# Early expert's w1: second halves of the columns split at the early slot instead of during attention; first tile's last low-part products moved

## The chip, the cores and the metric

One of the eight cores of a Trainium2 chip runs the kernel. The metric is the device time of one execution in microseconds (us), the median of three runs, lower being better. TensorE (PE) multiplies, VectorE (DVE), ScalarE (ACT) and GpSimd (POOL) do the work on elements, SyncE (SP) issues most transfers.

## The reference

Attention with a soft cap on the scores, for 8 batches, 12 heads, 448 positions and a head width of 64, is followed by a layer of experts on the 3584 rows of 768 that it yields; each row goes through the one expert of eight that its gate picks.

```python
scores = cap * np.tanh(np.matmul(q, k.transpose(0, 1, 3, 2)) / 8 / cap)
attn = softmax(scores)
x = (attn @ v).transpose(0, 2, 1, 3).reshape(3584, 768)
logits = x @ w_gate + modality_bias[modality_id]
e_idx, gate_w = argmax(logits), max(softmax(logits))
out[e_idx == e] = gate_w * (relu(x @ w1[e]) @ w2[e])     # w1: 768 x 1024, w2: 1024 x 768
```

## The kernel before

All matrix operands are split into a high part in a short float format (a cast on ScalarE) and the low rest (a subtraction on VectorE), and each product is made of three: high by high, high by low, low by high.

Attention (`attention`, L446) goes through 24 quads of four heads, three to a batch, each in four stages r = 0 to 3; a hand-written table, `ORDER`, says which steps of which quad are issued in a stage, and ScalarE does seven tanh (L532) and seven exp (L539) in each quad. A 25th round (i = 24, table `LAST`) finishes the last quad. Beside this the rows found so far are routed (`route`, L223): gate values, then the rank of each row within its expert by a matmul over counts (L257), a position from it (`pos`, L271), and four indirect puts by GpSimd that write row numbers and gate values to a table in DRAM, `mapd` (L284).

After four batches the expert with most rows is picked: the early expert. Its first 384 rows, all found in batches 0 to 5, are gathered during attention, and its first weights w1 (six tiles of 128x1024) are loaded and split there too: `load_part`, `hi_part` and `lo_part` (L665 to L682) work on twelve half tiles of 128x512, in the order left half, right half of tile 0, then of tile 1 and so on. Ten are split in quads 14 to 23, one in each stage r = 1, the last two at i = 24 and in `before`.

So the experts' part can start with a slot of 384 rows while the last batch is still being routed: the early slot. A slot (`run_slot`, L973) is a first layer (`ffn1`, L917; eight steps f, each 18 products of 128x384 into one bank, then relu into `hh` on ScalarE and its rest `hl` on VectorE), and a second (`ffn2`, L948; for each of three tiles of 128 rows and two halves of the columns, eight f with three products each into one bank `py`, which ScalarE scales into `ot`). Step f of the first layer needs columns 128 f to 128 f + 127 of all six w1 tiles, f of the second needs w2 tile f. Between the steps of the early slot's first layer stand hooks: `before`, `last` and `ranks` finish the last batch and its routing, `order` makes the plan of the slots that follow (`slots`, L325: a chain of some fifty short VectorE operations from `cnt`, L333, to `metai`, L395, and on to `plani`, L431), and `load_w2` loads and splits w2 tiles. Raw tiles of 128x1024 rotate through four buffers, so a load waits for the subtraction of the tile four back. Three w2 tiles are loaded ahead of the slot (`nstage`).

When the puts have landed GpSimd reads the list of the next slot's rows (`mt`, L837) and gathers them (L853, three gathers); TensorE transposes them late in the early slot's second layer (L895). The next slot's w1 is loaded and split from the second tile of the second layer on. Names in the traces: `raw` an unsplit weight tile, `ah`/`al` the parts of w1, `bh`/`bl` those of w2. On SyncE loads stand in the order of the program; on VectorE, ScalarE and TensorE too where an instruction is given to `pin`, the others being placed by a scheduler.

## Time and profile before

| | before |
|---|---|
| median of 3 runs | 838.93 us (838.35 to 839.43) |
| the profiled execution's own time | 840.97 us |
| its span | 839.3 us |
| TensorE busy | 823.2 us (98%), 5605 instructions |
| ScalarE busy | 528.1 us (63%) |
| VectorE busy | 518.7 us (62%) |
| GpSimd busy | 131.0 us (16%) |
| loads | 151.98 MB, mean 181 GB/s |

The span is that of one profiled execution; around it lie 1.7 us that the profile does not show. A share of busy time is a mean over the attention, where VectorE and ScalarE are nearly as full as TensorE, and the experts' part, where they are half empty. Rows of a timeline give the start, the duration, the engine, the line, the operation with its tiles, and in brackets the idle time of the engine just before with what ended it.

### The profile page before, as it was taken

The numbers are of one execution on the slowest core, as the hardware profiler recorded it, in microseconds if no ns is written. First come the engines' busy times: TensorE is split into PE (matmuls) and PEld (weight loads), VectorE is DVE, ScalarE is ACT, GpSimd is POOL, SyncE is SP. The second block draws the span as 40 slices with busy tenths as digits, with TensorE's granted clock in tenths as the row PEclk, the third lists the DMA queues.
The fourth block names the chain that finished last, engine by engine and source line by source line (L and its number), as shares of the span: only waits on it lengthen the run. The fifth ranks groups of instructions, "written<-read, shape, count | busy, mean of one in ns | idle before, by whom it ended". The sixth has DMA issues, their size and how long they took to land. (4 is left out here: it accounts for less than half of the span.)

```text
span 839.3 us, 15177 instructions
## 1 busy us (share of the span) xinstructions
PE 823.2 (98%) x5605; PEld 647.6 (77%) x5605; DVE 518.7 (62%) x987; ACT 528.1 (63%) x693; POOL 131.0 (16%) x155
## 2 busy tenths in 40 slices
PE   8999999999999999999999999999999999999995
PEld 3445454454545454999999999999999999999984
DVE  7788989899999998855344453444534335326510
ACT  7999999999999998345344453434534245335610
POOL 1000212020202024235020020200202002011101
PEclk9999999999999999999999999999999999999999
DMA  6565574858585855668366461654716547138743
GB/s 204 156 208 176 188 202 163 227 150 235 164 244 160 241 166 127 176 184 270 151 190 225 127 232 61 212 197 144 244 56 209 176 145 249 58 109 269 248 181 117
DMA packets 54649, 151.98 MB, mean 181 GB/s; under 512 B 9752, under 2 KB 18720, under 8 KB 54562
## 3 DMA queue, kind: packets, MB, share of 16 engines
q1 hardware_dynamic: 45200, 117.78, 45.4%
q0 software_dynamic: 9216, 33.10, 11.4%
q8 instruction: 47, 0.77, 0.4%
q14 instruction: 40, 0.33, 0.1%
q10 hardware_dynamic: 146, 0.00, 0.0%
HBM read 113.91 MB, written 22.40 MB: 162 GB/s over the span
## 5 line engine op out<-in xcount | busy, mean ns | idle before, releaser
L532 ACT ACTIVATE th<-sc,isc 128x896 f32<-128x896 f32 x168 | 161.1, 1003 | 8.3 <-PE sc L518 5.2
L932 PE MATMUL ph<-x,ah 128*128 128x384 f32 (+1 forms) x480 | 156.5, 326 | 1.4 <-ACT ot L967 1.0
L936 PE MATMUL ph<-x,al 128*128 128x384 f32 (+1 forms) x480 | 155.8, 325 | 0.0
L933 PE MATMUL ph<-x,ah 128*128 128x384 f32 (+1 forms) x480 | 155.8, 325 | 0.0
L962 PE MATMUL py<-bh,hh 128*128 128x384 f32 x448 | 151.0, 337 | 0.0
L962 PE MATMUL py<-bh,hl 128*128 128x384 f32 x448 | 149.9, 334 | 0.0
L962 PE MATMUL py<-bl,hh 128*128 128x384 f32 x448 | 149.8, 334 | 0.0
L539 ACT ACTIVATE pt<-th,cabs 128x896 f32<-128x896 f32 x144 | 142.1, 1042 | 0.0
L942 ACT ACTIVATE hh<-ph 128x384 fp32r<-128x384 f32 (+1 forms) x80 | 37.4, 469 | 131.7 <-PE ph L936 122.3
L552 PE MATMUL xT<-pt,va 128*64 128x448 f32 x576 | 118.8, 548 | 0.7 <-DVE xs L652 0.7
L870 DVE TENSOR_TENSOR bl<-raw,bh 128x768 fp32r<-128x768 f32 x80 | 74.3, 956 | 60.6 <-ACT bh L869 56.8
L943 DVE SCALAR_TENSOR_TENSOR hl<-ph,hh 128x384 fp32r<-128x384 f32 (+1 forms) x80 | 42.0, 528 | 106.5 <-ACT hh L942 105.1
L967 ACT ACTIVATE ot<-py,mt 128x384 f32<-128x384 f32 x56 | 32.5, 581 | 98.8 <-PE py L962 59.6
L932 PEld LDWEIGHTS ph<-x,ah 128*128 128x128 f32 x480 | 90.2, 188 | 2.8 <-issue 1.3
L968 POOL DMA_INDIRECT out_dram<-ot,mt x28 | 32.2, 1150 | 380.7 <-ACT ot L967 354.8
L933 PEld LDWEIGHTS ph<-x,ah 128*128 128x128 f32 x480 | 90.2, 188 | 0.0
L936 PEld LDWEIGHTS ph<-x,al 128*128 128x128 f32 x480 | 90.2, 188 | 0.0
L870 DVE TENSOR_TENSOR al<-raw,ah 128x1024 fp32r<-128x1024 f32 x54 | 63.9, 1222 | 35.1 <-ACT ah L869 32.2
L962 PEld LDWEIGHTS py<-bh,hh 128*128 128x128 f32 x448 | 84.1, 188 | 1.2 <-issue 0.7
L962 PEld LDWEIGHTS py<-bl,hh 128*128 128x128 f32 x448 | 84.1, 188 | 0.0
L962 PEld LDWEIGHTS py<-bh,hl 128*128 128x128 f32 x448 | 84.1, 188 | 0.0
L552 PEld LDWEIGHTS xT<-pt,va 128*64 128x64 f32 x576 | 37.1, 136 | 60.8 <-issue 51.4
(201 smaller groups left out, 1211.1 us busy)
## 6 DMA issues: line engine op xcount, KB each, us to landing
raw<-in_w_dram SPq DMA_DIRECT2D x86, 384.0 KB
raw<-in_w_dram SPq DMA_DIRECT2D x60, 512.0 KB
kq<-in_kq_dram SPq DMA_DIRECT2D x47, 448.0 KB
va<-in_v_dram SPq DMA_DIRECT2D x24, 448.0 KB
xd<-xs POOLq DMA_DIRECT2D x24, 448.0 KB
cp<-xT SPq DMA_DIRECT2D x44, 224.0 KB
cp<-gl SPq DMA_DIRECT2D x22, 224.0 KB
raw<-in_w_dram SPq DMA_DIRECT2D x12, 256.0 KB
```

What stands on the lines that cost most here:

```text
L532: pin(nc.scalar.activation(th, sc[:, :, :S], AF.Tanh, scale=self.isc))
L539: pin(nc.scalar.activation(e, th, AF.Exp, scale=self.cabs))
L552: pin(pe.matmul(xT[j * D : (j + 1) * D, :S], va[:, u * D : (u + 1) * D], quads[q]["pt"][t, i][:, j], start=t == i == 0, stop=t == 1 and i ...
L870: b = self.nc.vector.tensor_tensor(lo, raw, hi, op=ALU.subtract)
L932: nc.tensor.matmul(ph[:, :w], hi[:, fs], self.x[k][:, 0, :w], start=first, stop=False)
L933: nc.tensor.matmul(ph[:, :w], hi[:, fs], self.x[k][:, 1, :w], start=False, stop=False)
L936: nc.tensor.matmul(ph[:, :w], lo[:, fs], self.x[k][:, 0, :w], start=False, stop=last)
L942: nc.scalar.activation(hh[:, f, :w], acc, AF.Relu)
L943: nc.vector.scalar_tensor_tensor(hl[:, f, :w], acc, 0.0, hh[:, f, :w], op0=ALU.max, op1=ALU.subtract)
L962: nc.tensor.matmul(py[:, :HALF], self.h[a][:, f, rows], self.w2s[f][c][:, cs], start=i == 0, stop=i == 3 * FC - 1,)
L967: nc.scalar.mul(ot[:, cs], py[:, :HALF], mt[:, t, 1:2])
L968: self.last_out = nc.gpsimd.indirect_dma_start(self.out, bass.IndirectOffsetOnAxis(ap=mt.bitcast(I32)[:, t, 0:1], axis=0), ot, None, bound ...
```

## The change

In attention only the six left halves of the w1 tiles are loaded and split, in quads 15, 16, 18, 19, 21 and 22 (`PARTS`); quads 14, 17, 20 and 23 do nothing of it. The right halves are loaded after quad 23, two to a raw tile, and split at i = 24 and in the hooks `before`, `last` and a new one, `behind`. The rank matmul of the last batch moves from behind step f = 2 to behind f = 4. One w2 tile is loaded ahead in place of three; the others are loaded from the hooks behind f = 3 and 4 on.

In the second layer, the first tile of every slot makes the high-by-low products (w2's low part) of f = 5, 6 and 7 of its first half not in their place, but behind nine products of the other half; both banks are open meanwhile.

```diff
@@ -662,24 +662,31 @@
                     )
 
 
+            def part(n):
+                k, late = n % KC, n // KC
+                src = raws[KC + k // 2][:, k % 2 * 512 : k % 2 * 512 + 512] if late else raws[k]
+                return src, (t[:, late * 512 : late * 512 + 512] for t in self.w1s[k])
+
             def hi_part(n):
-                k, cs = n // 2, slice(n % 2 * 512, n % 2 * 512 + 512)
-                pin(nc.scalar.copy(self.w1s[k][0][:, cs], raws[n]))
+                src, (hi, lo) = part(n)
+                pin(nc.scalar.copy(hi, src))
 
             def lo_part(n):
-                k, cs = n // 2, slice(n % 2 * 512, n % 2 * 512 + 512)
-                hi, lo = self.w1s[k]
-                pin(nc.vector.tensor_tensor(lo[:, cs], raws[n], hi[:, cs], op=ALU.subtract))
+                src, (hi, lo) = part(n)
+                pin(nc.vector.tensor_tensor(lo, src, hi, op=ALU.subtract))
 
             def early_lo(i):
-                if 0 <= i - FIRST < 2 * KC - 2:
-                    lo_part(i - FIRST)
-
-            def load_part():
-                k, cs = len(raws) // 2, slice(len(raws) % 2 * 512, len(raws) % 2 * 512 + 512)
-                raw = self.up.tile([128, FF], F32, name="raw", tag="raw", bufs=RAWS)[:, :512]
-                self.load(raw, self.w1[ds(e, 1), k * 128 : (k + 1) * 128, cs].rearrange("o p f -> (o p) f"))
-                raws.append(raw)
+                if i in PARTS:
+                    lo_part(PARTS.index(i))
+
+            def load_parts(*ks, late=0):
+                raw = self.up.tile([128, FF], F32, name="raw", tag="raw", bufs=RAWS)
+                for n, k in enumerate(ks):
+                    self.load(
+                        raw[:, n * 512 : n * 512 + 512],
+                        self.w1[ds(e, 1), k * 128 : (k + 1) * 128, late * 512 : late * 512 + 512].rearrange("o p f -> (o p) f"),
+                    )
+                raws.append(raw if late else raw[:, :512])
 
             ORDER = (
                 ((group, 0, (None,)), (pvs, -1), (tot1, -1, 1), (xs, -1, 0), (tot2, -1, 1)),
@@ -708,7 +715,7 @@
                 ((den, -2),),
             )
             PICK, KNOWN = 3, 6
-            FIRST = PICK * NH + 5
+            PARTS = [PICK * NH + u for u in (6, 7, 9, 10, 12, 13)]
             WAYS = {(NQ - 2, 2): B - 2, **{(b * NH + 4, 3): b for b in range(B - 2)}}
             STEPS = [
                 (NQ - 2, 3), *((NQ - 1, r) for r in (0, 0, 1, 1)),
@@ -763,26 +770,35 @@
                         self.early_full(self.ps_r)
                         early = e, self.rows(meta, 0)
                         self.gather(early[1], known=KNOWN * S)
-                    if r == 1 and 0 <= i - FIRST < 2 * KC - 2:
-                        hi_part(i - FIRST)
-                    if r == 1 and 0 <= i - FIRST + 1 < 2 * KC:
-                        load_part()
+                    if r == 1 and i in PARTS:
+                        hi_part(PARTS.index(i))
+                    if r == 1 and i + 1 in PARTS:
+                        load_parts(PARTS.index(i + 1))
                     if (i, r) == (NQ - 1, 3):
                         self.make_x()
+                        for k in range(0, KC, 2):
+                            load_parts(k, k + 1, late=1)
                     if (i, r) == (NQ, 1):
                         self.split_x(*moved[1])
                         self.split_x(*turn_two(4, 5))
-                        hi_part(2 * KC - 2)
-                        lo_part(2 * KC - 2)
+                        hi_part(KC)
+                        hi_part(KC + 1)
+                        lo_part(KC)
+                    if (i, r) == (NQ, 2):
+                        for n in (1, 2):
+                            hi_part(KC + n + 1)
+                            lo_part(KC + n)
             self.raws = [self.load_raw(e, self.w2, k, DM) for k in range(self.nstage)]
 
             def before():
-                hi_part(2 * KC - 1)
+                hi_part(KC + 4)
+                hi_part(KC + 5)
                 tp(NQ - 2, 0)
                 tp(NQ - 2, 1)
                 lt(NQ - 1)
                 rows(NQ - 2, 0)
                 rows(NQ - 2, 1)
+                lo_part(KC + 3)
                 den(NQ - 1)
                 way(B - 1)
 
@@ -791,15 +807,18 @@
                 tp(NQ - 1, 1)
                 for _ in range(3):
                     next(routing[0])
+                lo_part(KC + 4)
+
+            def behind():
+                lo_part(KC + 5)
                 rows(NQ - 1, 0)
                 rows(NQ - 1, 1)
 
             def ranks():
                 for _ in range(2):
                     next(routing[0], None)
-                lo_part(2 * KC - 1)
-
-            return early, ((0, before), (1, last), (2, ranks))
+
+            return early, ((0, before), (1, last), (2, behind), (4, ranks))
 
 
     def moe_pools(self, st):
@@ -951,20 +970,24 @@
         for t in range(n):
             ot = self.lp.tile([128, C * 256], F32, name="ot", tag="late", bufs=3)[:, :DM]
             rows = slice(t * 128, (t + 1) * 128)
-            for half in range(2):
+            steps = [[(half, f, a, c) for f in range(FC) for a, c in ((0, 0), (0, 1), (1, 0))] for half in range(2)]
+            if t == 0:
+                late = [(0, f, 0, 1) for f in range(FC - 3, FC)]
+                steps = [[step for step in steps[0] if step not in late] + steps[1][:9] + late, steps[1][9:]]
+            py, left = [None, None], [3 * FC, 3 * FC]
+            for half, f, a, c in steps[0] + steps[1]:
+                if a == c == 0 and (2 * t + half, f) in at:
+                    at[2 * t + half, f]()
+                if py[half] is None:
+                    py[half] = self.ps_y.tile([128, 512], F32, name="py")
                 cs = slice(half * HALF, (half + 1) * HALF)
-                py = self.ps_y.tile([128, 512], F32, name="py")
-                i = 0
-                for f in range(FC):
-                    if (2 * t + half, f) in at:
-                        at[2 * t + half, f]()
-                    for a, c in ((0, 0), (0, 1), (1, 0)):
-                        nc.tensor.matmul(
-                            py[:, :HALF], self.h[a][:, f, rows], self.w2s[f][c][:, cs],
-                            start=i == 0, stop=i == 3 * FC - 1,
-                        )
-                        i += 1
-                nc.scalar.mul(ot[:, cs], py[:, :HALF], mt[:, t, 1:2])
+                left[half] -= 1
+                nc.tensor.matmul(
+                    py[half][:, :HALF], self.h[a][:, f, rows], self.w2s[f][c][:, cs],
+                    start=left[half] == 3 * FC - 1, stop=left[half] == 0,
+                )
+                if left[half] == 0:
+                    nc.scalar.mul(ot[:, cs], py[half][:, :HALF], mt[:, t, 1:2])
             self.last_out = nc.gpsimd.indirect_dma_start(
                 self.out, bass.IndirectOffsetOnAxis(ap=mt.bitcast(I32)[:, t, 0:1], axis=0), ot, None,
                 bounds_check=NT - 1, oob_is_err=False,
@@ -1252,7 +1275,7 @@
     def build(self):
         tc, nc = self.tc, self.nc
         with ExitStack() as st:
-            self.nstage = RAWS - 1
+            self.nstage = 1
             self.cpool = st.enter_context(tc.tile_pool(name="cpool", bufs=1))
             dram = st.enter_context(tc.tile_pool(name="dram", bufs=1, space=DRAM))
             self.plani = self.cpool.tile([1, 3], I32, name="plani")
@@ -1275,7 +1298,7 @@
                             self.meta = self.slots(rt, self.ps_r, True)
 
                         w2 = lambda at, *ks: (at, lambda: self.load_w2(early[0], self.raws, range(*ks)))
-                        self.run_slots(early, (*late, w2(2, 0, 4), (3, order), *(w2(f, f, f + 1) for f in range(4, FC))))
+                        self.run_slots(early, (*late, w2(3, 0, 2), (3, order), w2(4, 2, 4), *(w2(f, f, f + 1) for f in range(4, FC))))
                 with branch.Else():
                     self.general()
                     self.tail(fresh=True)
```

VectorE, early slot, before: the last rows of the ranks, then four low parts of w2 (bl, f = 0 to 3), then the start of the plan chain (cnt).

```order
L269 TENSOR_REDUCE posf<-rows 112x4
L271 CAST pos<-posf 112x4
L870 TENSOR_TENSOR bl_4497<-raw,bh_4496 128x768
L870 TENSOR_TENSOR bl_4499<-raw,bh_4498 128x768
L870 TENSOR_TENSOR bl_4501<-raw,bh_4500 128x768
L870 TENSOR_TENSOR bl_4503<-raw,bh_4502 128x768
L943 SCALAR_TENSOR_TENSOR hl<-ph,hh 128x384
L333 COPY cnt<-cps 128x8
```

VectorE at the same place with the change: the start of the plan chain (bl_4487 and bl_4489 are f = 0 and 1).

```order
L333 COPY cnt<-cps 128x8
L341 SCALAR_TENSOR_TENSOR left<-blkj,cnt 128x80
L962 SCALAR_TENSOR_TENSOR hl<-ph,hh 128x384
L342 TENSOR_SCALAR mask<-left 128x8x10
L344 TENSOR_REDUCE nbig<-mask 128x8
L889 TENSOR_TENSOR bl_4487<-raw,bh_4486 128x768
L889 TENSOR_TENSOR bl_4489<-raw,bh_4488 128x768
L346 SCALAR_TENSOR_TENSOR rem<-nbig,cnt 128x8
```

The chain now starts ahead of f = 0 and 1, and the rows of the ranks stand within it: pos is row 36 from cnt, metai row 59. At the chain's end, with the change (bl_4491, bl_4493, bl_4495 are f = 2, 3, 4):

```order
L393 TENSOR_SCALAR meta<-meta 128x1
L422 TENSOR_TENSOR plan<-plan,few 128x1
L426 TENSOR_SCALAR fits<-plan 128x1
L395 CAST metai<-meta 128x4
L889 TENSOR_TENSOR bl_4491<-raw,bh_4490 128x768
L427 TENSOR_TENSOR plan<-plan,fits 128x1
L428 MEMSET plan 128x1
L889 TENSOR_TENSOR bl_4493<-raw,bh_4492 128x768
L431 CAST plani<-plan 1x3
L889 TENSOR_TENSOR bl_4495<-raw,bh_4494 128x768
```

The low parts of f = 2 and 3 have moved from ahead of cnt to behind metai.

TensorE, second layer of the early slot, first half of the first tile with the change, from the high product of f = 5 (bh_4496) to the first products of the other half (bh_4486 is f = 0).

```order
L985 MATMUL py<-bh_4496,hh 128x384
L985 MATMUL py<-bh_4496,hl 128x384
L985 MATMUL py<-bh_4498,hh 128x384
L985 MATMUL py<-bh_4498,hl 128x384
L985 MATMUL py<-bh_4500,hh 128x384
L985 MATMUL py<-bh_4500,hl 128x384
L985 MATMUL py<-bh_4486,hh 128x384
```

The products with the low parts of f = 5, 6 and 7 (bl_4497, bl_4499, bl_4501) are gone from here; they follow behind nine products of the other half.

ScalarE, first slot of two tiles, before: the evictions `ot` of the first tile and the casts of the next w1.

```order
L942 ACTIVATE hh<-ph 128x256
L869 CAST ah_155<-raw 128x1024
L869 CAST ah_157<-raw 128x1024
L869 CAST ah_159<-raw 128x1024
L967 ACTIVATE ot<-py,mt 128x384
L869 CAST ah_161<-raw 128x1024
L967 ACTIVATE ot<-py,mt 128x384
```

With the change:

```order
L961 ACTIVATE hh<-ph 128x256
L888 CAST ah_155<-raw 128x1024
L888 CAST ah_157<-raw 128x1024
L888 CAST ah_159<-raw 128x1024
L888 CAST ah_161<-raw 128x1024
L990 ACTIVATE ot<-py,mt 128x384 x2
```

The first `ot` has moved behind the cast of the last w1 tile.

## Rows read from the trace of the kernel before

**Rows 1.** Windows, steady attention: us, busy PE, PEld, DVE, ACT, POOL; PEclk, DMA share, GB/s.

```profile
100.00:200.00 100.00, 99.95 (x773) 49.40 (x767) 91.51 (x188) 97.00 (x106) 19.08 (x22) 1.00 0.64 181
```

**Rows 2.** Windows, early slot and just ahead of it.

```profile
332.00:338.00 6.00, 6.00 (x49) 2.73 (x42) 4.64 (x9) 4.13 (x10) 0.44 (x2) 1.00 0.72 64
...
348.40:349.40 1.00, 1.00 (x8) 0.96 (x8) 0.97 (x4) 0.12 (x1) 0.00 (x0) 1.00 0.09 18
...
354.00:356.00 2.00, 2.00 (x14) 2.00 (x13) 1.90 (x6) 0.18 (x1) 1.48 (x2) 1.00 1.10 335
...
356.00:359.00 3.00, 3.00 (x19) 3.00 (x18) 2.96 (x22) 1.21 (x3) 0.94 (x1) 1.00 0.73 84
...
359.00:361.00 2.00, 2.00 (x14) 2.00 (x13) 2.00 (x20) 1.16 (x2) 0.00 (x0) 1.00 0.68 236
```

**Rows 3.** Timeline of TensorE, early slot: counts, second layer's start, next transposes.

```profile
352.38 0.18 PE L298 MATMUL cps<-acc,ones 112*128 112x8 bf16 x1
...
364.98 0.34 PE L962 MATMUL py<-bh,hh 128*128 128x384 f32 x1
...
385.81 0.29 PE L895 MATMUL xt<-identr,xg 128*128 128x128 f32 x2
```

**Rows 4.** Timeline of VectorE, early slot: ranks, low parts of w2, plan chain.

```profile
350.83 0.17 DVE L271 CAST pos<-posf 112x4 int32<-112x4 f32 x1
...
350.91 3.63 DVE L870 TENSOR_TENSOR bl<-raw,bh 128x768 fp32r<-128x768 f32 x4
...
354.93 0.15 DVE L333 COPY cnt<-cps 128x8 f32<-128x8 f32 x1
...
361.91 0.16 DVE L395 CAST metai<-meta 128x4 int32<-128x4 f32 x1
```

**Rows 5.** Timeline of SyncE: two issues of weight loads.

```profile
348.37 0.33 SPq L93 DMA_DIRECT2D raw<-in_w_dram  x1
...
390.77 0.33 SPq L93 DMA_DIRECT2D raw<-in_w_dram  x1
```

**Rows 6.** Timeline of GpSimd: early slot's third gather, first and last put, mt, gather.

```profile
323.51 1.00 POOL L853 DMA_INDIRECT xg<-xd,mt  x1 [0.30 <-issue]
...
351.81 0.99 POOL L284 DMA_INDIRECT mapd<-pay,pos  x1 [0.93 <-DVE pos L271]
...
356.09 0.94 POOL L284 DMA_INDIRECT mapd<-pay,pos  x1 [0.30 <-issue]
...
363.84 0.61 POOL L837 DMA_DIRECT2D mt<-mapd  x1 [6.81 <-DMA mapd<-pay,pos]
...
374.56 1.00 POOL L853 DMA_INDIRECT xg<-xd,mt  x1 [0.30 <-issue]
```

**Rows 7.** Timeline of ScalarE: a cast behind its load; last w1 cast, first two-tile slot.

```profile
394.66 0.84 ACT L869 CAST bh<-raw 128x768 fp32r<-128x768 f32 x1 [2.34 <-DMA raw<-in_w_dram]
...
779.09 1.05 ACT L869 CAST ah<-raw 128x1024 fp32r<-128x1024 f32 x1 [1.31 <-DMA raw<-in_w_dram]
```

**Rows 8.** Timeline of ScalarE, attention: the same exp at two pairs of batch boundaries.

```profile
127.86 1.04 ACT L539 ACTIVATE sh<-th,cabs 128x896 f32<-128x896 f32 x1
...
168.38 1.05 ACT L539 ACTIVATE sh<-th,cabs 128x896 f32<-128x896 f32 x1
...
250.32 1.04 ACT L539 ACTIVATE sh<-th,cabs 128x896 f32<-128x896 f32 x1
...
291.15 1.04 ACT L539 ACTIVATE sh<-th,cabs 128x896 f32<-128x896 f32 x1
```

**Rows 9.** Groups of instructions, 15 to 340 us: weights split during attention (busy, mean ns).

```profile
L667 ACT CAST ah<-raw 128x512 fp32r<-128x512 f32 x11 | 6.8, 614 | 0.0
...
L672 DVE TENSOR_TENSOR al<-raw,ah 128x512 fp32r<-128x512 f32 x11 | 7.6, 689 | 0.0
```

**Rows 10.** Timeline of TensorE: early slot's own transposes; two-tile slot's second tile.

```profile
330.28 0.36 PE L904 MATMUL sc<-identr,xg 128*128 128x128 f32 x2
...
780.33 0.41 PE L962 MATMUL py<-bh,hh 128*128 128x384 f32 x1
```

## The prediction

> **What bounds the kernel now.** I read the page's busy line first (it stands in the table above): TensorE is busy for 823.2 us of a span of 839.3, so only what makes TensorE wait, or what takes a wait from it, can move the time. A window over the steady attention comes next [rows 1]: in 100 us TensorE idles for 0.05, beside ScalarE at 97.0% and VectorE at 91.5%. TensorE is always at work there, yet its products go into banks that ScalarE's tanh and exp set free, so two engines are near the edge. The windows over the early slot show TensorE at 2.00 of 2.00 and 3.00 of 3.00 us [rows 2]: nothing makes it wait there, so the change can take no wait away in that slot and can only add one. What is left to read is the moment by which each thing that the change makes later is wanted: TensorE's timeline for the want [rows 3], and those of VectorE, SyncE, GpSimd and ScalarE for the supply [rows 4 to 7].
>
> **Attention: four ScalarE casts fewer.** A batch of three quads takes ScalarE 168.38 − 127.86 = 40.52 us where no weight is cast, and 291.15 − 250.32 = 40.83 where three casts are [rows 8]. Three casts cost 0.31, so one costs 0.10, though each is 0.614 long [rows 9]: the rest falls into ScalarE's small gaps, the 3.0% of rows 1. Ten casts stood in quads 14 to 23, six stand there now; four fewer give **−0.4 us**. Bounds: 0, if the 0.31 is the spread of a batch, and −4 × 0.614 = −2.46, if ScalarE alone sets the pace and a cast comes back whole. I take the measured batch difference, the nearest row. VectorE's subtractions that go with the casts (0.689 each [rows 9]) I cost at nothing: VectorE has 8.5% to spare there and TensorE is full beside it.
>
> **The second halves, now split around the early slot's start.** Six casts of 0.614 are 3.7 us of ScalarE, six subtractions of 0.689 are 4.1 us of VectorE. The four steps f = 4 to 7 of the first layer take 364.98 − 352.38 = 12.6 us [rows 3], 3.15 a step of 18 products, 0.175 a product. The upper half of the weights' columns is first used at f = 4, at 352.4; casts and subtractions lie in the last attention stages and in the 12.6 us of f = 0 to 3, beside TensorE: **0**. Without that cover each late subtraction would cost its 0.69. The six half loads go out ahead of the w2 loads, and one w2 tile is loaded ahead instead of three; the other two go out as half tiles are split, over 10 us before the second layer: 0.
>
> **The second layer's last weights.** This is the term that decides. Before, VectorE did four low parts of w2 (f = 0 to 3) at 350.91 to 354.54, ahead of the plan chain, which starts at 354.93 with the copy to cnt and ends with metai at 361.91 [rows 4]. In the changed order only those of f = 0 and 1 stand between the chain's first rows; those of f = 2 and 3 stand behind metai. The raw tiles rotate through four buffers, so the load of f = 6 goes into the buffer that the low part of f = 2 frees, and f = 7 into that of f = 3. The chain's start hangs on the matmul of the counts at 352.38 [rows 3], so cnt comes at about 352.6. From cnt to metai it took 6.98 us. To this I add one low part more, 3.63 / 4 = 0.91, one hl more (half as wide, 0.46), and 0.4 for the four rows of the ranks that now stand inside the chain, at 0.11 a row (53 rows in 6.98 us, one hl and one low part among them: 5.6 / 51). That is 8.75, so metai comes at 361.4. The low part of f = 2 then ends at 362.4 and that of f = 3 at 363.3, and these are the issues of the last two loads; before, both buffers were free by 354.54.
>
> How long do the loads take? A load issued at 390.77 [rows 5] was cast at 394.66 [rows 7]: 3.9 us. But these two now run beside the four indirect puts of the ranks to DRAM, which the change makes later too. pos now stands 23 rows ahead of metai, 23 × 0.11 = 2.5 us, so at 358.9 instead of 350.83 [rows 4]. The first put follows pos by 0.98, and the last starts 4.28 after the first [rows 6]: 359.9 to 364.2. Around the puts the load rate falls: 335 GB/s as the last one was started (354 to 356), 84 over the next 3 us, then 236; and 64 over 6 us behind the puts of the batch before [rows 2]. I lay the first three windows, 8.1 us later, over the two loads of 393 KB each. Bytes begin some 1.1 us behind an issue (18 GB/s in the first microsecond behind that of 348.37 [rows 2, 5]), at 363.5: 0.7 us at 335 GB/s bring 235 KB, 3 us at 84 bring 252, and the last 299 KB at 236 take 1.3. So f = 6 has landed at 366.1 and f = 7 at 368.5. From landing to cast I take 1.1 us (3.9, less 1.1 to the first byte, less 1.7 for 393 KB at 236 GB/s) and for a cast 0.85 [rows 7]: ScalarE has f = 6 done at 368.05 and f = 7 at 370.45. TensorE starts the second layer at 364.98 [rows 3]; with the low products of f = 5 to 7 put off, it wants f = 6 behind 17 products, at 367.95, and f = 7 behind 19, at 368.3. It waits 0.1 and then 2.05, in all **+2.2 us**. Bounds: at 3.9 us from issue to cast it is 0.2 (f = 7's cast ends at 368.5, behind that of f = 6 and one hh); at 64 GB/s for all the bytes f = 7 is cast by 363.5 + 12.3 + 1.95 = 377.75, a wait of 9.5. I take 2.2, since its three windows follow puts at the distance at which the loads will follow them.
>
> The reordered low products (f = 5 to 7 of the first half behind nine of the other) want the low part of f = 7 at 372.5, and it is ready one subtraction behind its cast, at 371.4: no second wait. Without this reorder the same loads would cost about 1 us more.
>
> **The next slot's rows.** The plan's row list is read back once the puts have landed. The load of mt was issued 7.75 us behind the last put's start (363.84 − 356.09), and the third gather 10.7 later (374.56) [rows 6]. From 364.2 that gives 372.0 and 382.7, ending 383.7. The early slot's own third gather was issued by 324.51 [rows 6] and its rows were transposed at 330.28 [rows 10]: it lands within 5.8, here by 389.5. The transposes, due at 385.81 [rows 3], come at 388.0 with the +2.2 above. A wait of 0 to 1.5; I take **+0.4**, the low third, since the 5.8 holds more than the landing. Bounds 0 and 389.5 − 385.81 = 3.7, the latter with no wait ahead of it.
>
> **The reorder in the other slots.** As many products in another order, and in rows of a full TensorE no wait for a low part to save: 0. But a slot's first ot is ready nine products later, and in ScalarE's order it then stands behind the last cast of the next weights. In the first slot of two tiles that cast starts at 779.09 and takes 1.05 [rows 7], so the two ot of tile 0 end at 780.6 or later, while the first product of the next tile, at 780.33 [rows 10], wants the first one's bank: **+0.3**, between 0 and 0.5.
>
> **Sum.** −0.4 + 2.2 + 0.4 + 0.3 = +2.5 us. The profiled execution took 840.97 itself, 2.04 above the median of the runs; its span would go from 839.3 to 841.8, the median from 838.93 to **841.4 us**. What a measurement can tell from no change is 0.2%, 1.7 us.
>
> **Rivals.**
> *The puts don't hold the loads up.* Then f = 6 and 7 are cast 3.9 us behind their issue: −0.4 + 0.2 + 0.8 (the gathers, with hardly a wait ahead) + 0.3 = +0.9, **839.8**. For it: the 335 GB/s while the last put was being started [rows 2]. Against it: the 84 and 64 behind them, though less may have been asked for there. The Trainium skill, "DMA: Bandwidth & Descriptors", "Queues, rings and completion order", has a rule on this side: each DMA engine takes turns between queue rows packet by packet, so that a put's few small packets would leave a load nearly its rate. By that rule this rival holds, and the 84 GB/s row does not agree with it. Chance 0.27.
> *ScalarE alone paces attention.* A cast then comes back whole, and if the loads are on time as well the time is −2.46 + 0.2 + 0.3 = −2.0, **836.9**: faster. It decides from a gain of about 0.55 us for each cast taken out (4 × 0.55 − 0.5 = 1.7). For it: ScalarE's 97%, above VectorE's 91.5 [rows 1]. Against it: 0.31 for three casts [rows 8]. Chance 0.09.
> *The low rate lasts.* 64 GB/s held for 6 us behind the puts before [rows 2]; if it holds while both loads are under way, f = 7 comes 5 to 9.5 us late and the gathers hide behind that: −0.4 + 5 to 9.5 + 0.3, **844 to 848**. Against it: in those 6 us little may have been waiting. Chance 0.12.
>
> **How the numbers follow.** The forecast has 0.52 and a range of its own of 840.8 to 843.5. That lies above 840.6, where slower begins; 0.52 with the third rival's 0.12, less 0.04 for a forecast whose terms all fall low, is 0.60. Same has 0.31: the first rival, and that 0.04. Faster keeps the second rival's 0.09. The range takes in the first rival from 838.6 (its gathers on time, its cast gain doubled) and the lower third of the last one, up to 845.0; it leaves out the second and the rest of the third.
>
> **What would show it.** In the profile after: metai near 361.4; two load issues at 362 to 364 in SyncE's timeline; the first put at about 360; TensorE idle before the second layer's f = 6 and 7, some 2.2 us between 367.5 and 371, its releaser the casts; the first layer's start some 0.4 earlier. It is wrong if those casts are done before TensorE asks, if the low parts of f = 2 and 3 run before metai, or if attention gets shorter by over 1 us.

## The result and the profile after

The changed kernel takes 844.22 us (842.96 to 846.17, 6 runs), the kernel before, measured beside it, 838.51: a ratio of 1.0069 (95% interval 1.0056 to 1.0082), 5.7 us slower. The forecast was 841.4, in a range from 838.6 to 845.0.

The page of the changed kernel begins:

```profile
span 843.7 us, 15190 instructions
...
PE 825.4 (98%) x5605; PEld 650.0 (77%) x5605; DVE 518.5 (61%) x987; ACT 529.0 (63%) x693; POOL 133.1 (16%) x155
```

Its own time was 845.31 us. What TensorE waited for from 363 to 398 us, a stretch in which the kernel before had no wait (engine, line waited for: us in all, times, longest):

```profile
PE xt L914 <- DMA xg<-xd,mt: 2.3, 2, 1.7
PE py L985 <- ACT bh L888: 1.8, 2, 1.3
```

TensorE's timeline has the places: the start of the early slot's second layer, the first products that need the casts of f = 6 and 7, the transposes of the next rows, the first product behind them, and the starts of the next slot's first and second layer.

```profile
363.96 0.34 PE L985 MATMUL py<-bh,hh 128*128 128x384 f32 x1
...
368.44 0.45 PE L985 MATMUL py<-bh,hh 128*128 128x384 f32 x1 [1.34 <-ACT bh L888]
...
369.56 0.44 PE L985 MATMUL py<-bh,hh 128*128 128x384 f32 x1 [0.49 <-ACT bh L888]
...
387.37 0.22 PE L914 MATMUL xt<-identr,xg 128*128 128x128 f32 x1
388.14 0.28 PE L914 MATMUL xt<-identr,xg 128*128 128x128 f32 x1 [0.55 <-DMA xg<-xd,mt]
390.17 1.56 PE L914 MATMUL xt<-identr,xg 128*128 128x128 f32 x16 [1.75 <-DMA xg<-xd,mt]
...
391.57 0.41 PE L985 MATMUL py<-bh,hh 128*128 128x384 f32 x1
...
397.39 0.34 PE L951 MATMUL ph<-x,ah 128*128 128x384 f32 x1
...
422.35 0.34 PE L985 MATMUL py<-bh,hh 128*128 128x384 f32 x1
```

The early slot's second layer, 364.98 [rows 3] to 391.54 before, now runs from 363.96 to 397.39: 33.43 us in place of 26.56, **+6.87**. In parts: 2.58 up to the first transpose, 2.71 over the transposes, and 1.58 in the last 24 products, which take 5.82 us in place of 4.24. The brackets give idle time; from start to start the two waits for casts cost 2.16 of the 2.58 (the rest are slower products beside them), and the two waits for gathered rows 2.63 of the 2.71. No wait explains the last 24 products; the windows do (columns as in rows 1):

```profile
361.00:366.00 5.00, 5.00 (x31) 5.00 (x30) 3.31 (x6) 0.49 (x1) 2.33 (x2) 1.00 0.79 36
...
366.00:368.00 2.00, 1.10 (x7) 0.78 (x5) 0.00 (x0) 0.44 (x1) 0.00 (x0) 1.00 0.96 373
...
389.00:390.00 1.00, 0.00 (x0) 0.00 (x0) 0.00 (x0) 0.00 (x0) 1.00 (x1) 1.00 0.82 203
...
392.00:395.00 3.00, 3.00 (x11) 3.00 (x11) 3.00 (x7) 2.91 (x6) 1.04 (x1) 0.51 0.02 6
```

TensorE is full from 392 to 395 and does 11 products, with a granted clock of 0.51, the lower of its two levels (1.2 of 2.4 GHz), behind the idle time at 387.6 to 390.2. (The two windows of 361 to 368 are for the loads, further below.)

All else is the same or shorter: the first layer of the early slot 27.57 us (27.55 before), the next slot's first layer 24.96 (25.63 before, with a wait for an hl that is gone: 0.40 idle, 0.56 from start to start), and from there to the last product 411.23 us in both. So between these two traces the whole loss lies in one second layer of one slot, +6.87 − 0.67 = +6.2, and the attention, 1.04 shorter in this trace, makes it 5.18 at the last product. The spans differ by 4.4 because the profile before had 0.75 us more behind its last product, in a pause of GpSimd (rows at e11).

What made it late: first the rows of VectorE, then those of GpSimd, to be read beside rows 4 and 6.

```profile
351.42 0.17 DVE L333 COPY cnt<-cps 128x8 f32<-128x8 f32 x1 [0.28 <-PE cps L298]
...
357.24 0.15 DVE L271 CAST pos<-posf 112x4 int32<-112x4 f32 x1
...
359.62 0.16 DVE L395 CAST metai<-meta 128x4 int32<-128x4 f32 x1
359.69 0.95 DVE L889 TENSOR_TENSOR bl<-raw,bh 128x768 fp32r<-128x768 f32 x1
```

```profile
358.20 1.05 POOL L284 DMA_INDIRECT mapd<-pay,pos  x1 [6.09 <-DVE sel L384]
...
362.70 0.94 POOL L284 DMA_INDIRECT mapd<-pay,pos  x1 [0.30 <-issue]
373.06 1.75 POOL L856 DMA_DIRECT2D mt<-mapd  x3 [9.43 <-DMA mapd<-pay,pos]
...
382.48 2.05 POOL L872 DMA_INDIRECT xg<-xd,mt  x1 [0.30 <-issue]
```

pos comes 6.4 us later than before, the last put starts 6.6 later (356.09 [rows 6]), but the list of rows is read 9.2 later and the third gather is issued 7.9 later. The gather's own issue took 2.05 us; it took 1.00 before. The last two w2 loads were issued at 360.67 and 361.61, the last three puts from 359.56 on. Views of DMA issues (count, KB each, median us from issue to landing), for the loads and puts from 360 to 363 us, and for the gathers from 378 to 392 us:

```profile
raw<-in_w_dram SPq DMA_DIRECT2D x2, 384.0 KB, 6.9
...
mapd<-pay,pos POOLq DMA_INDIRECT x3, 9.1
```

```profile
xg<-xd,mt POOLq DMA_INDIRECT x3, 7.6
```

### The profile page after: what moved, and what is told of

Its sections match the earlier page's. It is cut to its first block, busy times and chain, and to the rows that moved or that the text cites. A ratio compares the mean times of both kernels' runs of the same rounds, so it can differ in the third digit from the quotient of the medians.

```text
span 843.7 us, 15190 instructions
## 1 busy us (share of the span) xinstructions
PE 825.4 (98%) x5605; PEld 650.0 (77%) x5605; DVE 518.5 (61%) x987; ACT 529.0 (63%) x693; POOL 133.1 (16%) x155
## 5 line engine op out<-in xcount | busy, mean ns | idle before, releaser
L985 PE MATMUL py<-bl,hh 128*128 128x384 f32 x448 | 147.3, 336 | 0.0
L888 ACT CAST bh<-raw 128x768 fp32r<-128x768 f32 x80 | 64.2, 833 | 33.5 <-DMA raw<-in_w_dram 31.4
```

The lines of the kernel that those rows point to most:

```text
L888: a = self.nc.scalar.copy(hi, raw)
L985: nc.tensor.matmul(py[half][:, :HALF], self.h[a][:, f, rows], self.w2s[f][c][:, cs], start=left[half] == 3 * FC - 1, stop=left[half] == 0,)
```

## The experiments

Each is the changed kernel with the edit shown, unless it says otherwise. "Before" is the kernel before, measured beside it on the same chip; e1 to e4 ran on one chip, e5 to e8 on a second, e9 to e11 on a third, e12 on a fourth.

**e1: ranks back behind f = 2.**

```diff
-            return early, ((0, before), (1, last), (2, behind), (4, ranks))
+            return early, ((0, before), (1, last), (2, ranks), (2, behind))
```

> The changed kernel with the rank matmul of the last batch back behind step f = 2 (ahead of behind); all else as changed. VectorE's order then has pos ahead of cnt again and the low parts of f = 2 and 3 inside the chain. Theory (the late puts carry the loss: they make the gathers late and lie over the last two loads): first put near 352, no wait of the second layer for its casts, no wait of the transposes for the gathers, granted clock 1.00 throughout; attention's gain of 1.2 us stays, so about 837.5 us, faster than the kernel before by 1. Rival (the loss comes from the late right halves and the w2 tiles loaded later, the puts only stand beside): the casts of f = 6 and 7 are still waited for, 1 us or more, and the time is 839 to 841.

Measured: 840.10 us, before 838.88, ratio 1.0014 (1.0005 to 1.0022). Some 4.5 of the 5.7 us are gone, with both waits and the fall of the clock. One new wait is there, which neither theory had. TensorE's waits from 363 to 398, and the row on VectorE that leads to it:

```profile
PE py L985 <- DVE hl L962: 0.7, 1, 0.7
```

```profile
361.65 0.96 DVE L889 TENSOR_TENSOR bl<-raw,bh 128x768 fp32r<-128x768 f32 x1 [2.75 <-ACT bh L888]
```

With the ranks out of the chain, the scheduler puts the low part of f = 4 inside it; its load was issued at 354.02 beside the puts and landed some 6.7 us later, at 360.76, and VectorE stood still for 2.75 us, with the plan and the hl behind that low part in its order.

**e2: low parts of f = 2 and 3 ahead of the chain's middle, ranks late as changed.**

```diff
-  ... w2(3, 0, 2), (3, order), w2(4, 2, 4), ...
+  ... w2(3, 0, 4), (3, order), ...
```

> The changed kernel with w2 tiles 2 and 3 split in the hook of f = 3 ahead of the plan, so their low parts stand ahead of the chain's middle and the loads of f = 6 and 7 go out some 4 us earlier; the ranks stay behind f = 4, the puts 1 to 2 us later than in the changed kernel. Theory (late puts): the wait for casts goes (1.8 to 0), but the gathers are as late as before or later, their wait grows from 2.3 to 3 to 5 us and the clock falls again: 842.5 to 845 us, no real gain. Rival (the released buffers decide, and the puts are slow only because the loads run beside them): both waits go, 837.5 to 839 us.

Measured: 842.95 us, before 838.88, ratio 1.0052 (1.0036 to 1.0068). The wait for casts is gone, the one for gathers has grown, and the clock falls again:

```profile
PE xt L914 <- DMA xg<-xd,mt: 2.9, 2, 1.5
```

```profile
388.00:390.00 2.00, 1.65 (x14) 1.65 (x14) 0.77 (x2) 1.29 (x4) 0.43 (x1) 0.61 0.61 229
390.00:392.00 2.00, 2.00 (x10) 2.00 (x10) 2.00 (x5) 1.41 (x4) 0.69 (x1) 0.54 0.00 0
```

TensorE came to the transposes 2.4 us earlier (384.94 for 387.37) and stood there longer; it went on with the last gather's rows at 388.35, 1.8 earlier than in the changed kernel (390.17), and the median is 1.3 us lower than the changed kernel's, 1.6 if each is taken against its own before. Late gathers, a wait for them and the slower clock are the theory's case, and the rival, that the buffers decide, falls. One thing the theory had wrong: the gathers came earlier, not as late as before or later.

**e3: puts early, low parts of f = 2 to 5 behind metai.** e1's edit, and

```diff
-  ... w2(4, 2, 4), *(w2(f, f, f + 1) for f in range(4, FC))
+  ... w2(5, 2, 5), w2(5, 5, 6), *(w2(f, f, f + 1) for f in range(6, FC))
```

> Ranks back behind f = 2, but w2 tiles 2 to 5 split from the hook of f = 5 on, so the low parts of f = 2 and 3 stay behind metai as in the changed kernel: puts early, last loads late. Theory (puts lying over the loads make them slow): the two loads take about 4 us from issue to landing instead of 6.9, the wait for casts is under 0.5 us, no wait for gathers: 837.5 to 838.3 us. Rival (late buffers alone): the loads still take 6 us or more, the wait for casts stays 1.5 to 2 us, 839 to 840 us.

Measured: 840.72 us, before 838.88, ratio 1.0027 (1.0017 to 1.0036). In its profile there is no wait for gathers and the clock stays at 1.00, but the casts are still waited for, 0.49 and 0.13 us, and the two loads, issued at 361.53 and 362.46, are between the two expectations (DMA issues of 361 to 363 us):

```profile
raw<-in_w_dram SPq DMA_DIRECT2D x2, 384.0 KB, 5.2
```

So without the puts the loads take 1.7 us less than the 6.9; at 5.2 they are still slower than the 3.9 reckoned with, now beside the reads of the row list. The two waits cost 0.95 us from start to start, less than the 1.8 that the median lost: seven of the twelve runs lie between 839.7 and 841.0, five between 841.7 and 842.8, and what the five had more is not shown by this profile.

**e7: transposes twelve products later, puts late as changed.**

```diff
-  at = {(2, 0): lambda: self.load_w1(nxt[0]), (5, 0): every}
+  at = {(2, 0): lambda: self.load_w1(nxt[0]), (5, 4): every}
```

> The changed kernel with the transposes of the next rows twelve products later, ahead of f = 4 of the last half in place of f = 0, 2.1 us; puts as late as in the changed kernel. Theory (when the third gather lands, at 390, sets the end, and the idle time ahead of it lets the clock fall): TensorE comes to the transposes at 389.5, waits under 0.8 us, the granted clock stays 1.00, and the time is 2.5 to 3.5 us less than the changed kernel's, 841 to 841.7 us. Rival (the wait for casts, 1.8 us, is what is lost, the gathers only move along with it): 0 to 0.5 us less, 843.7 to 844.2 us.

Measured: 842.02 us, before 839.14, ratio 1.0037 (1.0025 to 1.0050): 2.9 above before, where the changed kernel was 5.7 above. The waits of 363 to 398, and the windows just ahead of and in the changed kernel's stretch at the lower clock:

```profile
PE py L985 <- ACT bh L888: 1.7, 2, 1.2
```

```profile
390.00:392.00 2.00, 2.00 (x18) 2.00 (x17) 1.23 (x2) 1.65 (x4) 0.00 (x0) 1.00 1.01 373
392.00:395.00 3.00, 3.00 (x19) 2.92 (x18) 3.00 (x8) 2.93 (x6) 1.76 (x2) 1.00 0.87 268
```

Puts, loads and casts as in the changed kernel, but no wait for rows and, in this profile, no fall of the clock. So late gathers, with what they do to the clock, are up to half of the loss. How much is not sharp: the profile is the second fastest of six runs, two of the others have a mean clock of 0.994 (0.996 in this one), and beside e5, which has the changed kernel's slot and ran on the same chip, e7 is only 0.8 us faster.

**e4, e5 and e10: attention's third cast and subtraction.** In quads 17, 20 and 23 the half tile of the quad before is cast again (e4, the second pair of lines), subtracted again (e5, the first pair), or both (e10).

```diff
+                elif i - 1 in PARTS:
+                    lo_part(PARTS.index(i - 1))
...
+                    if r == 1 and i - 1 in PARTS and i not in PARTS:
+                        hi_part(PARTS.index(i - 1))
```

> The changed kernel with three casts done once more, in quads 17, 20 and 23 (the same half tile cast again), so that those batches hold three casts as before the change; their subtractions are not repeated. Theory (ScalarE's gaps hold two casts of a batch for nothing, the third makes ScalarE the bound and costs 0.31 us): 3 x 0.31 = 0.9 us longer attention than the changed kernel, the three quads' exps 0.3 us later each; 845.1 us. Rival (each cast costs 0.10, as the prediction had it): 0.3 us longer. Rival (the gain came from VectorE's subtractions): nothing changes.

> The changed kernel with three subtractions done once more in quads 17, 20 and 23 (the same half tile again), the casts as in the changed kernel. The third cast alone gave attention nothing back (its exps of quad 23 came at the same time as in the changed kernel). Theory now (VectorE's subtractions made the batches longer: three of 0.69 us in a batch take it from 91.5% to its bound, two do not): 0.2 to 0.3 us a batch, the exps of quad 23 0.6 to 0.9 us later, 844.8 to 845.1 us. Rival (cast and subtraction only cost together, or the gain lies elsewhere, in the earlier start of the loads for instance): no change, 844.2 us.

> The changed kernel with cast and subtraction both done once more in quads 17, 20 and 23. Theory (only both together fill those quads: the cast delays the exps, the subtraction the xs for which TensorE waits 0.21 to 0.25 us in these quads in the profile before): TensorE's wait for xs is back in the three quads, the exps of quad 23 come 0.8 to 1.1 us later than in the changed kernel, 845 to 845.3 us. Rival (the gain was one execution's, or the loads' that stood in these quads): no wait for xs, the same exps within 0.2 us.

Measured: e4 844.63, before 838.88, ratio 1.0069 (1.0055 to 1.0082); e5 842.85, before 839.14, 1.0047 (1.0034 to 1.0060); e10 847.94, before 840.76, 1.0088 (1.0074 to 1.0102). The last exp but those of the last round, on ScalarE's timeline, stood at 318.50 in the profile before and at 317.31 in the changed kernel's; in e4, e5 and e10 (one fence each):

```profile
317.34 1.05 ACT L539 ACTIVATE sh<-th,cabs 128x896 f32<-128x896 f32 x1
```

```profile
317.30 1.04 ACT L539 ACTIVATE sh<-th,cabs 128x896 f32<-128x896 f32 x1
```

```profile
318.59 1.05 ACT L539 ACTIVATE sh<-th,cabs 128x896 f32<-128x896 f32 x1
```

Alone neither lengthens attention by more than 0.03 us; both theories of a single bound fall. With both, TensorE waits for xs again (200 to 320 us of e10):

```profile
PE xT L552 <- DVE xs L652: 0.9, 3, 0.5
```

That agrees with e10's theory, but does not show it, for a reason that stands at e11.

e4 also shows the price of the clock: it waits in the early slot as the changed kernel does (1.8 for casts, 2.5 for gathers), and in its profile the clock did not fall:

```profile
392.00:395.00 3.00, 3.00 (x20) 3.00 (x19) 3.00 (x6) 3.00 (x6) 1.19 (x1) 1.00 0.02 6
```

20 products in place of 11 in the same 3 us. Its last product ends at 832.02, the changed kernel's at 833.58: 1.56 us, the price of the clock, once more. In e5's profile, with nearly the same idle time at the transposes as e4's (1.05 and 1.26 us there, 1.04 and 1.41 here), it did fall:

```profile
390.00:392.00 2.00, 1.87 (x15) 1.87 (x15) 0.95 (x3) 1.47 (x4) 0.48 (x1) 0.50 0.87 303
392.00:395.00 3.00, 3.00 (x13) 3.00 (x12) 2.54 (x6) 2.28 (x5) 1.05 (x1) 0.50 0.05 18
```

That profile, at 846.22 us, is the longest of e5's five runs (842.43 to 846.22).

**e6 and e9: the reorder of the second layer.** e6 is e3 with the products in the order of before; e9 is the kernel before with the new order alone (the change's lines in the second layer, nothing else).

> The kernel of e3 (ranks behind f = 2, w2 tiles 2 to 5 split from f = 5 on), but with the second layer's products in their order of before. In e3 the casts of f = 6 and 7 are waited for by 0.95 us together, no gather is. Theory (the put-off products spare TensorE the wait for the low parts of f = 6 and 7, one subtraction behind their casts): TensorE waits 0.7 to 1 us more than in e3, 841.4 to 841.7 us. Rival (the reorder gives nothing, since with the low products in place TensorE comes to the casts of f = 6 and 7 two and four products later, 0.35 to 0.5 us, and gets that back): the same as e3 within 0.4 us.

> The kernel before with the second layer's reorder alone (low products of f = 5 to 7 of a slot's first half-tile behind nine of the other half); attention, w1 and the ranks as before. Theory (the reorder moves work of the same size and frees nothing where no low part is waited for): no change, 838.5 to 839.3 us, and no new wait at the second tile of a two-tile slot. Rival (the first ot, nine products later and behind the last cast of the next w1, is waited for, as the prediction's 0.3 had it): 0.3 us in each two-tile slot, 839.2 us.

Measured: e6 841.87, before 839.14, ratio 1.0033 (1.0020 to 1.0046); e9 841.00, before 840.76, ratio 1.0003 (0.9994 to 1.0012). In e6 TensorE waits twice for low parts, f = 6 and 7 (363 to 398 us), where e3 has one longer wait left, 0.5:

```profile
PE py L981 <- DVE bl L889: 1.1, 2, 0.6
```

By their traces the waits cost 1.83 us in e6 and 0.95 in e3 from start to start, so the reorder spares 0.9 where the loads are late, as its theory had it. The medians, 2.7 and 1.8 us above their own before, differ by as much, but their intervals overlap, and they hold something else too: in e6's profile the clock fell behind these waits (0.51 from 370 to 373 us), in e3's it did not. In e9, where nothing is late, it is worth nothing. The wait for an ot bank is not there: in the first slot of two tiles the second tile follows the second layer's start by 9.31 us in e9 (770.33 to 779.64), in the changed kernel (776.19 to 785.50) and before (771.02 to 780.33 [rows 10]).

**e8 and e12: puts early, and nothing in the chain that waits for a load.** e1's edit, and

```diff
-  ... w2(4, 2, 4), *(w2(f, f, f + 1) for f in range(4, FC))
+  ... w2(4, 2, 4), w2(6, 4, 7), *(w2(f, f, f + 1) for f in range(7, FC))
```

> Ranks behind f = 2 as in e1, but w2 tiles 4 to 6 split in the hook of f = 6, so that the low part of f = 4, for whose load VectorE stood still 2.75 us in e1, comes behind metai and no hl behind it; the low parts of f = 2 and 3 stay inside the chain, so the last two loads go out near 358. Theory (with the puts early and nothing in VectorE's order waiting for a load, all waits of the early slot go): TensorE idles 0 to 0.3 us in the slot, attention keeps its 1.1 us, 837.5 to 838.2 us, a little less than the kernel before. Rival (the later split of the right halves has its price all the same, since the w2 loads lie beside the puts): casts of f = 4 to 7 are late by 0.5 to 1.5 us, 838.5 to 840 us.

> The kernel of e8 once more, with a fresh comparison. Theory (TensorE's 0.2 us waits for xs in attention are gone and nothing waits in the early slot): 0.5 to 1.2 us less than the kernel before. Rival (the gain in attention is taken back where e8's first comparison does not show it): within 0.3 us of the kernel before, as in e8.

Measured: e8 838.94, before 839.14, ratio 1.0000 (0.9992 to 1.0009); e12, the same kernel, 838.59, before 838.69, ratio 0.9999 (0.9990 to 1.0008). All of the loss is gone; of TensorE's waits from 336 to 398 us a single one is left in both, before a matmul of the ranks, which the kernel before has too:

```profile
PE rank L259 <- DVE before L252: 0.2, 1, 0.2
```

But it is not faster than the kernel before, though its trace shows no wait for xs in attention and its exp of quad 23 at 317.16.

**e11: the kernel before, a second profile.**

> The kernel before, unchanged, for a second profile, since its first one was 2 us above its median. Theory (attention's gain of 1.2 us is the change's): TensorE waits again 0.2 us for xs in quads 17, 20 and 23, the exps of quad 23 at 318.5, and what made the first profile 2 us long lies elsewhere. Rival (that execution's attention was long by chance): the waits are missing, the exps of quad 23 come at 317.4 or so, and the change gains nothing in attention; then also the kernel of e8, which has no wait in the early slot, has no reason to be faster than the kernel before, as its median says.

Measured: 840.40, and 840.76 for the other runs of the same kernel on that chip; the exp of quad 23 stands at 318.21, and TensorE waits for xs twice, 0.4 us. The theory's rows are there. Yet the chip of e9 to e11 ran the kernel before 1.6 to 2.3 us slower than the others did (838.5 to 839.1), and its profiles share a second mark with the first profile of before, the pause of GpSimd ahead of its last put. First the profile before, then e10 (a changed kernel, on that chip), then e8:

```profile
831.35 0.98 POOL L1089 DMA_INDIRECT out_dram<-of,index  x1 [1.06 <-POOLq L1125]
```

```profile
839.33 0.98 POOL L1116 DMA_INDIRECT out_dram<-of,index  x1 [1.05 <-POOLq L1152]
```

```profile
829.28 0.98 POOL L1112 DMA_INDIRECT out_dram<-of,index  x1 [0.32 <-POOLq L1148]
```

So all four profiles with the wait for xs (before, e9, e10, e11) also have this longer pause, whichever kernel they are of, and none of the others has either. Whether attention's 0.9 to 1.2 us come from the change or from where these four ran was not told apart: that needed the kernel before profiled on one of the other chips. Two things narrow it. That chip is not slower in attention as such: e10 does what the changed kernel does up to quad 16, and up to there the two keep pace; the same exp as above stands in quad 16 at 222.86 in e10 and at 222.74 in the changed kernel:

```profile
222.86 1.04 ACT L539 ACTIVATE sh<-th,cabs 128x896 f32<-128x896 f32 x1
```

```profile
222.74 1.04 ACT L539 ACTIVATE sh<-th,cabs 128x896 f32<-128x896 f32 x1
```

From there to the exp of quad 23 e10 takes 95.73 us and the changed kernel 94.57, so the 1.2 us arise where e10 has its third cast and subtraction. And e8 and e12 lose nothing in the early slot and are within 0.1% of before, so on their chips attention gained at most 0.7 to 0.8 us.

## Why the prediction held, and where it didn't

**What bounds, and where the change can act: right.** The early slot had no wait to give, and the loss arose there: e8 and e12, which wait for nothing new there, lose nothing.

**Attention, −0.4: open.** −1.04 at the first layer's start between the two traces, just beyond the 1 us that the prediction named as a sign of being wrong; but e8 and e12 leave 0 to −0.8 in the medians. The step "three casts cost 0.31, so one costs 0.10" rests on ScalarE's gaps alone, and e4 shows that a third cast alone costs nothing in the attention. VectorE's subtractions, which the sum put at nothing, cost nothing alone either (e5); what the two cost together on the other chips is not shown.

**The second halves, 0: right.** 27.57 against 27.55 us for the first layer with all its hooks.

**The second layer's last weights, +2.2: right in the path, near in size by luck.** The waits for the casts of f = 6 and 7 cost 2.16 from start to start, and 2.58 with the slower products beside them. The path was the one described: metai, two low parts, two loads that lay beside the puts, two casts. The first cast on ScalarE:

```profile
367.56 0.83 ACT L888 CAST bh<-raw 128x768 fp32r<-128x768 f32 x1 [6.03 <-DMA raw<-in_w_dram]
```

metai came 1.8 us earlier than reckoned (359.62 for 361.4): cnt was 1.2 earlier, with the whole slot, and the chain 0.55 shorter (8.20 for 8.75). The loads took 6.9 us each from issue to landing where the windows of before had given 3.7 and 5.2. The two errors stood against each other. The parts show it: a wait of 0.1 for f = 6 and of 2.05 for f = 7 was forecast; from start to start it was 1.5 and 0.66. The load rate had another course too: 36 GB/s from 361 to 366 and 373 behind that, in place of 335, 84 and 236.

The first rival, loads at their own rate, fell: 36 GB/s from 361 to 366 at a DMA share of 0.79. What the prediction drew for it from the Trainium skill ("DMA: Bandwidth & Descriptors", "Queues, rings and completion order": each DMA engine takes turns between queue rows packet by packet), a load at nearly its own rate, does not agree with these 36 GB/s. But e3 shows that without the puts the two loads still take 5.2 us, so the puts are not all of it.

**The next slot's rows, +0.4: the step that failed.** It cost 2.63. The issue of the third gather came where it was reckoned, at 382.48 for 382.7, by two errors against each other: the last put started 1.5 us early (362.70 for 364.2), and the list of rows was read 10.36 behind it (362.70 to 373.06), not 7.75 as before. (It was 9.11 in e2, and 6.99 and 7.32 in e3 and e8, where the puts were early: puts that come late also land late.) What failed is the landing. The issue took 2.05 us in place of 1.00, and the rows came 5.6 behind its end, at 390.17; the "low third" of the wait had them at 388.4, and 389.5 was given as the latest. That latest rests on one gather before, 5.8 us, and is no bound: from the issue's end to the last transposes it was 6.3 to 7.9 us in e2, e4, e5 and e10. TensorE, for its part, came to the transposes at 387.37 and not 388.0.

And the two waits are not additive, as the sum had them: where the last gather's landing sets the end, the wait for casts ahead of it is partly cover. In e2 it is gone, and TensorE stands at the gathers for the longer; in e7 the transposes stand behind the landing and wait for nothing. Adding a third of the one to the other gave +2.6 for the two terms where the traces have 2.58 + 2.71.

**Not in the sum: the clock, +1.6.** No term and no rival had it. e4 shows it apart: with the same slot and no fall its last product ends 1.56 us earlier. In e7's profile, without the last wait, it does not fall.

**Not in the sum: a wait that went, −0.67.** The next slot's first layer lost 0.56 to a wait for an hl before, and nothing now. Before, ScalarE stood until 402.23 for the load of a w2 tile, 10.7 us behind the layer's start, and hh and hl came behind that cast; now it stands until 405.87, but that is 8.5 us behind the later start.

**The reorder: right in both halves.** 0 elsewhere (e9), about 0.9 where the loads are late (e6), for which the prediction had about 1. The +0.3 for the ot bank was wrong: 9.31 us from the second layer's start to the second tile in all three, so 0.

The sum of the terms was +2.5, or +2.9 without attention; the traces' is 2.58 + 2.71 + 1.58 − 0.67 = +6.2 without attention, and the medians say +5.7. The range reached to 845.0 for another reason, a low load rate that lasts (the third rival); that mechanism did not occur as described: a low rate came, but it ended at 366, and both casts together were waited for by 2.2 us, not 5. That 844.2 lies in the range is luck.

## What to carry to other kernels

Before moving a step back in a full stretch, follow everything that it issues to its last consumer: here a rank matmul two steps later cost nothing where it stood, and some 4.5 us (e1) further on, much of it at the gathers, three transfers later. Waits in a row on one engine don't add up: find the one whose end is fixed by something else (the landing of the last gather), and count the others only where they go beyond it. And a wait at TensorE should be priced with what may follow it: 1.6 us at half clock behind 2.3 us of idle time, in some executions and not in others.

## What was not expected of the hardware

In the profiles the granted clock fell to its lower level in the changed kernel (behind idle times of 0.55 and 1.75 us, then full work), in e2 (1.33 and 1.52), e5 (1.05 and 1.26) and e10 (1.94 and 1.53), and in e6 behind 0.14, 0.56 and 0.54. It did not fall in e4 (1.04 and 1.41) nor in e7 (1.22 and 0.49). So nearly the same idle time was followed by a fall in e5 and by none in e4, and what decides is open. The mean granted clock of each run points the same way: it is 0.996 to 0.998 in the 76 runs of the kernel before beside e1 to e12, and in all runs of e1, e8, e9, e11 and e12; lower values, 0.993 to 0.995, are found only in kernels that wait in the slot for casts, low parts or gathers, in some of their runs. It does not order the changed kernel's runs by time, though: its fastest, 842.96, has the lowest clock, 0.994.

The four puts of the ranks took 6.4 to 7.75 us from the last one's start to the list's read when they began near 351 (e1 aside, where the read waited for VectorE), and 9.1 to 10.4 when they began near 358 to 360, beside the last w2 loads. Which of the two holds up the other is not settled: removing the puts from under the loads gave the loads 1.7 us, and moving the loads ahead of the puts (e2) gave the puts 1.2.
